# Block 0's second product: two of W_out's four slices as seven products of halves, and the first product in column halves

## The chip, the cores and the metric

The kernel runs on one core of a Trainium2 chip. The core has five engines that run side by side and wait for each other through semaphores: TensorE (PE in the profile; its weight loads are PEld), VectorE (DVE), ScalarE (ACT), GpSimd (POOL) and SyncE (SP), which here only issues DMAs. Each engine works through its own queue in order. The metric is the device time of one execution in microseconds.

## The reference

```python
# retention, for each of 4 batches x 8 heads, 768 tokens, head size 64
for t in range(S):
    state = gamma * state + outer(k[t], v[t])
    y[t] = scale * q[t] @ state
# then a feed-forward part over all 3072 tokens
x = y.transpose(0, 2, 1, 3).reshape(3072, 512)
h = x @ w_in                        # 512 -> 2048
g = h * tanh(softplus(h))           # the "mish" function
out = g @ w_out                     # 2048 -> 512, float32
```

Inputs and output are float32; the kernel computes its products on float16 copies.

## The kernel before

**Blocks.** The 3072 tokens are 24 chunks of 128. Block 0 has four chunks (512 tokens); every later block has two (256 tokens). For each block the kernel computes the retention part y, turns it into xt (the features on the partitions, the tokens in the columns), multiplies by W_in and applies mish (together `g1`), and multiplies by W_out. The retention part of the next block is computed by small products that are put between the large ones.

**Weights.** W_in and W_out arrive by DMA in four slices each, as float32, and are cast to float16 in SBUF. Slice s of W_out (`wout0` to `wout3`) holds the rows 512 s to 512 s + 511, as four row blocks of 128 (f = 0 to 3). The staging tiles are one ring of four buffers (tag "wt"): first the first q, then W_in's slices, then W_out's, and at last four tiles of sums, `tmat` (two) and `gsum` (two). Slices 0 to 2 of W_out are issued by `load_w`, one DMA of 1 MB each; slice 3 is issued in two halves by `load_last_wout`, out of `load_more`, after the loads of q, k and v for chunks 4 and 5. All of these stand in SP's queue in program order. `cast_wout` casts slices 0 to 2 on DVE (L220) and slice 3 on ACT in two halves (L218).

**Seven products.** From block 1 on, the second product is not computed plainly. Function `seven` splits the gate matrix g (256 tokens x 2048) and W_out (2048 x 512) into 2 x 2 parts each, a11 to a22 over halves of the tokens and of f, b11 to b22 over halves of f and of the columns. With s1 = a21 + a22, s2 = s1 - a11, s3 = a11 - a21, s4 = a12 - s2 and t1 = b12 - b11, t2 = b22 - t1, t3 = b22 - b12, t4 = b21 - t2, seven products (a11 b11, a12 b21, s1 t1, s2 t2, s3 t3, s4 b22, a22 t4) and some additions give the four parts of the result that eight products give otherwise. DVE makes the sums of g for each block (`gsum`, L699 to L708); the sums of the weights (`tmat`, `weight_sums`, L683 to L686) are made once, in two halves: half 0 from slices 0 and 2, half 1 from slices 1 and 3. In block 0 the kernel before makes them, but doesn't use them.

**Block 0.** Its order is written out by hand in the loop at L1076 and the dictionary `plan`: steps u = 0 to 15 are the first product, one row block of 128 of the 2048 features each. `open_in` does the first two; `g1` (L628) does the others with four products of 512 columns each (L635), and ACT applies mish on the finished bank (L643). Steps 16 to 31 are the second product: 64 products of 512 columns (`g2_mm`, L649), for each of 16 row blocks f one for each of the four token chunks t. Each of four PSUM banks (`o_ps`) gathers the sum of one token chunk over all of f. `g2_out` copies the banks out, bank 0 on ACT (L662), the others on DVE (L664), and the stores are issued in block 1.

Between them `plan` puts chunks 4 and 5 (called pair 2): `cast_qk` scales q and v on POOL (L297) and k on ACT (L293); `turn_two` turns q and k by 16 TensorE transposes (L247) into one PSUM tile, which DVE copies out in four pieces (L253); `pair_scores` does the scores of half the heads, twice, each with 16 small products (L327) and a mask on DVE (L332); `outer_two` does the outer products k v (L345) and the state (L358); `present_two` and `y_two` give y (L373, L383), whose two halves are copied to xt by DVE (L402) and ACT (L400). With that xt, block 1's first product starts. `turn_both` scales chunks 6 and 7 on POOL (L414, L417, L424), and SP turns them by DMA (L429) for block 1's small products.

PSUM has eight banks: four for the large products (one "px", three "mm") and two double ones ("at") for pair 2.

Of the kernel before, what the change touches and what calls it, by code (L numbers as in the profile page):

```python
# [9 lines left out]
FP16 = mybir.dt.float16  # L10
# [6 lines left out]
def kernel(  # L17
# [12 lines left out]
    P = 128  # L30
# [169 lines left out]
    def cast_win(s, by_tile=False):  # L200
        src = wtmps.pop(("in", s))
        wins[s] = []
        for j in range(2):
# [7 lines left out]
            wins[s].append(t)  # L211

    def cast_wout(s, on_act=False):
        src = wtmps.pop(("out", s))
        t = cpool.tile([P, FPS, d_model], FP16, name=f"wout{s}")
        if on_act:
            for f in range(0, FPS, 2):
                nc.scalar.copy(t[:, f:f + 2], src[:, f:f + 2])  # L218
        else:
            nc.vector.tensor_copy(t, src)  # L220
        wouts[s] = t

# [405 lines left out]
    def g1(blk, u):  # L628
# [3 lines left out]
        for j in range(per):  # L632
            s, f = divmod(u * per + j, FPS)
            for bp in range(NBP):
                nc.tensor.matmul(  # L635
                    h_ps[:, j], wins[s][f // 2][:, bp, f % 2 * P:(f % 2 + 1) * P], xts[blk][:, bp, :nt],
                    start=(bp == 0), stop=(bp == NBP - 1))
        room = NFB * TB // (2 * nt)
# [7 lines left out]

    def g2_mm(o_ps, blk, t, fb, cols=slice(None)):
        s, f = divmod(fb, FPS)
        nc.tensor.matmul(  # L649
            o_ps, gts[blk, fb][:, t * P:(t + 1) * P], wouts[s][:, f, cols],  # L650
            start=(fb == 0), stop=(fb == NFB - 1))

    def out_rows(blk, t):
# [4 lines left out]

    def g2_out(o_ps, t, due):
        osb = op.tile(list(o_ps.shape), FP32, name="osb", tag="osb")  # L660
        if t == 0:
            nc.scalar.copy(osb, o_ps)  # L662
        else:
            nc.vector.tensor_copy(osb, o_ps)  # L664
        stores.append((due, out_rows(0, t), osb))

    def weight_sums(half):
# [10 lines left out]
        t3, t4 = tmats[1][:, 0, f], tmats[1][:, 1, f]  # L678
        b11, b12 = wouts[half][:, :, :hf], wouts[half][:, :, hf:]
        b21, b22 = wouts[half + 2][:, :, :hf], wouts[half + 2][:, :, hf:]  # L680
        sub = ALU.subtract
# [28 lines left out]
    def in_sums(j):  # L710
        t = cpool.tile([P, 4, 2, TB // 2], FP16, name=f"wsum_{j}")
        wsums.append(t)
        (a11, a12), (a21, a22) = [(x[:, :2], x[:, 2:]) for x in (wins[0][j], wins[2][j])]
# [247 lines left out]
    def first_block():  # L961
# [82 lines left out]
        def turn_two():  # L1044
# [15 lines left out]

        plan = {
            9: [(cast_wout, 0)],
            12: [(cast_wout, 1)],
            16: [(cast_wout, 2), (load_more,), (cast_qk,)],
            17: [(sum_weights, 0, 3)],
            23: [(cast_wout, 3, True)],
            25: [(turn_two,)],
            26: [(pair_scores, 2, 0)],
            27: [(pair_scores, 2, 1)],
            28: [(sum_weights, 0, 1), (turn_both, CPB + 2)],  # L1070
            29: [(outer_two,)],
            30: [(present_two,), (sum_weights, 1, 1)],
            31: [(y_two,)],
        }
        o_tiles = [None] * CPB
        for u in range(2 * NFB):  # L1076
            if u < 2:
                if u == 0:
                    open_in(2)
            elif u < NFB:  # L1080
                g1(0, u)
            elif u < 2 * NFB - 2:
                w = u - NFB
                if w == 0:
                    for t in range(CPB):
                        pool, tag = (pxps, "px") if t == 0 else (mmps, "mm")
                        o_tiles[t] = pool.tile([P, d_model], FP32, name="o_ps", tag=tag)
                for t in range(CPB):
                    if t == CPB - 1 and w == 1:
                        g2_mm(o_tiles[t], 0, t, 0)  # L1090
                    if t < CPB - 1 or w > 0:
                        g2_mm(o_tiles[t], 0, t, w)
            else:
                for t in range(CPB // 2) if u % 2 == 0 else range(CPB // 2, CPB):
                    for w in range(NFB - 2, NFB):
                        g2_mm(o_tiles[t], 0, t, w)
                    g2_out(o_tiles[t], t, 0)
            for fn, *args in plan.get(u + 1, ()):
                fn(*args)

# [171 lines left out]
```

## Time and profile before

| | us |
|---|---|
| median of 3 runs | 196.34 (196.23 to 196.53) |
| the profiled execution | 196.27 |
| its span, first to last instruction | 194.5 |
| TensorE busy | 189.6 |
| granted TensorE clock, mean | 0.998 |
| block 0's first product in `g1`, 56 products | 19.34 to 31.42 |
| block 0's second product, pair 2 in it | 31.42 to 48.74 |

In the profile a row gives the start in us from the span's beginning, the time it took, the engine, the line in the kernel, the operation, the tiles it writes and reads, their shapes, how many instructions are merged in the row, and in square brackets the idle time before it with what ended it. TensorE pipelines its products: a row of 512 columns reads 380 ns, but the next starts 216 ns later, so costs are taken from start to start.

### The profile page before, as it was taken

How to read it: one execution, taken by the hardware profiler on the slowest of the kernel's cores; microseconds unless marked ns; L12 is line 12 of the kernel's file. 1: busy time of each engine (PE TensorE's matmuls, PEld its weight loads, DVE VectorE, ACT ScalarE, POOL GpSimd, SP SyncE). 2: the span in 40 equal slices, each digit the busy share in tenths (PEclk: the TensorE clock that was granted, in tenths of full speed). 3: DMA queues.
4: the chain of work that ended last, by engine and by line, in shares of the span. 5: the costliest groups of instructions: out<-in, count | busy, mean ns of one | idle time of the engine just before them, and what ended most of it. 6: DMA issues, size and time to landing. Idle time of an engine off the chain costs nothing.

```text
span 194.5 us, 6886 instructions
## 1 busy us (share of the span) xinstructions
PE 189.6 (97%) x2996; PEld 154.0 (79%) x2996; DVE 128.7 (66%) x248; ACT 99.5 (51%) x183; POOL 73.3 (38%) x96
## 2 busy tenths in 40 slices
PE   7998999999999999999999999999999999999994
PEld 7756444454888888888888888998998998988983
DVE  0796535889767378467884864965885885876462
ACT  3375764243553552554364364584574663763750
POOL 5262000549508746562826605525625700000000
PEclk9999999999999999999999999999999999999999
DMA  5999999999999999999999999889996250300202
GB/s 172 304 309 349 368 386 366 293 302 202 202 260 248 157 233 225 214 175 216 261 207 227 278 192 287 103 225 245 77 223 123 50 150 5 111 0 20 95 27 81
DMA packets 84285, 38.75 MB, mean 199 GB/s; under 512 B 57760, under 2 KB 78880, under 8 KB 84256
## 3 DMA queue, kind: packets, MB, share of 16 engines
q1 hardware_dynamic: 84112, 38.28, 84.7%
q8 instruction: 23, 0.38, 0.9%
q10 hardware_dynamic: 144, 0.05, 0.1%
q14 instruction: 6, 0.05, 0.1%
HBM read 27.31 MB, written 6.29 MB: 173 GB/s over the span
## 4 chain that ended last, share of the span: by engine, by line
PE 93%; DMA 3%; ACT 1%; DVE 1%; issue 1%; SPq 0%
PE o_ps L838 32%; PE h_ps L635 24%; PE h_ps L765 9%; PE h_ps L745 8%; PE o_ps L649 7%; PE y_ps L551 3%; DMA qfirst<-in_q_dram 3%; PE u_ps L479 1%; PE at L472 1%; PE t_ps L247 1%; PE y_ps L373 1%; PE h_ps L620 1%; PE at L443 1%; PE at L327 1%; DVE qk L259 1%
## 5 line engine op out<-in xcount | busy, mean ns | idle before, releaser
L635 PE MATMUL h_ps<-xt,win 128*128 128x256 f16 (+1 forms) x376 | 48.5, 289 | 0.0
L635 PEld LDWEIGHTS <-win 128*128 128x128 f16 x376 | 36.5, 98 | 10.4 <-issue 0.2
L643 ACT ACTIVATE g<-h_ps 128x512 f16<-128x512 f32 x54 | 32.2, 597 | 23.7 <-PE h_ps L635 23.7
L838 PEld LDWEIGHTS <-gsum 128*128 128x128 f16 x320 | 30.3, 98 | 3.8
L838 PE MATMUL o_ps<-tmat,gsum 128*128 128x256 f16 x240 | 29.8, 273 | 0.0
L838 PEld LDWEIGHTS <-g 128*128 128x128 f16 x248 | 23.4, 98 | 2.7
L853 DVE TENSOR_TENSOR osb<-o_ps,snap 128x256 f32<-128x256 f32 (+1 forms) x33 | 13.8, 418 | 14.0 <-PE o_ps L838 8.9
L844 ACT COPY snap<-o_ps 128x256 f32<-128x256 f32 (+1 forms) x33 | 12.2, 370 | 20.7 <-PE o_ps L838 20.7
L414 POOL TENSOR_TENSOR qk<-qf,qvs 128x512 f16<-128x512 f32 x18 | 19.2, 1065 | 4.8 <-DMA qf<-in_q_dram 4.7
L765 PE MATMUL h_ps<-xt,win 128*128 128x256 f16 x160 | 20.7, 273 | 0.0
L424 POOL TENSOR_TENSOR v<-vf,qvs 128x512 f16<-128x512 f32 x18 | 19.7, 1101 | 1.2 <-DMA vf<-in_v_dram 1.0
L417 POOL TENSOR_TENSOR qk<-kf,qvs 128x512 f16<-128x512 f32 x18 | 19.1, 1060 | 2.7 <-DMA kf<-in_k_dram 2.6
L838 PE MATMUL o_ps<-wout,g 128*128 128x256 f16 x160 | 19.1, 273 | 0.0
L1179 POOL COPY summed<-gsum 128x1 f16<-128x1 f16 x7 | 3.0, 432 | 37.2 <-DVE gsum L704 29.8
L765 PEld LDWEIGHTS <-win 128*128 128x128 f16 x160 | 14.8, 98 | 1.4
L756 ACT ACTIVATE g<-h_ps 128x512 f16<-128x512 f32 x25 | 14.2, 588 | 2.4 <-PE h_ps L765 2.4
L600 ACT CAST xt<-y_ps 128x512 f16<-128x512 f32 x15 | 10.2, 734 | 10.2 <-PE y_ps L551 10.2
L649 PE MATMUL o_ps<-wout,g 128*128 128x512 f16 x64 | 15.0, 380 | 0.0
L780 DVE TENSOR_TENSOR hsum<-h_ps,hsum 128x512 f32<-128x512 f32 x15 | 10.4, 692 | 6.1 <-PE h_ps L745 4.4
L775 ACT COPY hsum<-h_ps 128x512 f32<-128x512 f32 x15 | 8.8, 585 | 10.5 <-PE h_ps L745 10.5
L699 DVE TENSOR_TENSOR gsum<-g 128x512 f16<-128x512 f16 x20 | 9.2, 459 | 5.2 <-ACT g L643 3.1
L507 DVE TENSOR_TENSOR mid<-u_ps,sth 128x256 f16<-128x256 f32 x15 | 6.3, 422 | 8.5 <-PE u_ps L479 8.2
(99 smaller groups left out, 277.7 us busy)
## 6 DMA issues: line engine op xcount, KB each, us to landing
kf<-in_k_dram SPq DMA_DIRECT2D x24, 256.0 KB, 5.3
vf<-in_v_dram SPq DMA_DIRECT2D x24, 256.0 KB, 5.5
out_dram<-osb SPq DMA_DIRECT2D x22, 256.0 KB, 3.5
qf<-in_q_dram SPq DMA_DIRECT2D x20, 256.0 KB, 4.3
wi<-in_moe_w_in_dram SPq DMA_DIRECT2D x6, 512.0 KB, 8.7
wt<-in_moe_w_out_dram SPq DMA_DIRECT2D x3, 1024.0 KB, 10.3
qfirst<-in_q_dram SPq DMA_DIRECT2D x2, 512.0 KB, 4.6
wi<-in_moe_w_in_dram SPq DMA_DIRECT2D x1, 1024.0 KB, 10.0
```

The costliest lines, as they stand in the source:

```text
L414: nc.gpsimd.tensor_tensor(in_place(q16.rearrange("p (w x) d -> p w x d", x=2)), by_head(qf), scale_by_head(qs_two[:, heads]), op=ALU.mult)
L417: nc.gpsimd.tensor_tensor(k16.rearrange("p (y w) d -> p w y d", y=2), kf.rearrange("p (w y) d -> p w y d", y=2), boosts.rearrange("p (w y) ...
L424: nc.gpsimd.tensor_tensor(cast[g][2], loaded.pop(g)[2], vs[g % 2].unsqueeze(2).broadcast_to((P, H, D)), op=ALU.mult)
L635: nc.tensor.matmul(h_ps[:, j], wins[s][f // 2][:, bp, f % 2 * P:(f % 2 + 1) * P], xts[blk][:, bp, :nt], start=(bp == 0), stop=(bp == NBP - 1))
L643: nc.scalar.activation(gt, h_ps, AF.Mish, scale=inv_boost3)
L649: nc.tensor.matmul(o_ps, gts[blk, fb][:, t * P:(t + 1) * P], wouts[s][:, f, cols], start=(fb == 0), stop=(fb == NFB - 1))
L745: nc.tensor.matmul(o_ps[:, f], w(f // 2, k)[:, f % 2 * P:(f % 2 + 1) * P], x[:, k], start=begin and f == 0 and k == 0, stop=k == 1, skip_g ...
L756: nc.scalar.activation(to, src, AF.Mish, scale=inv_boost3)
L765: nc.tensor.matmul(h_ps[:, f], wins[w][h // 2][:, k, h % 2 * P:(h % 2 + 1) * P], xts[blk][:, k, :2 * C], start=k == 0, stop=k == NBP - 1)
L838: nc.tensor.matmul(o_ps[:, cols], x(f), w(f)[:, cols], start=first and z == 0, stop=z == n - 1, skip_group_check=True)
L844: nc.scalar.copy(x, o_ps[:, cols])
L853: nc.vector.tensor_tensor(dst, o_ps[:, cols], plus, op=ALU.add)
```

## The change

Block 0's second product takes another form, with what serves it:

- `g1` issues its products in pieces of 256 columns. For later blocks, whose tiles are 256 wide, that is what it was; in block 0 each product becomes two, each with its own weight load.
- Slices 0 and 2 of W_out (f blocks 0 to 3 and 8 to 11) are multiplied by seven products, over halves of f (slice 0, slice 2), halves of the tokens (two chunks each) and halves of the columns. Slices 1 and 3 are multiplied plainly, in pieces of the same size. Every product or piece is 8 instructions of 256 columns (4 row blocks x 2 chunks).
- A PSUM bank now holds two chunks x 256 columns. Parts that are used twice are copied or added out of PSUM on the way (`kept_sum`: m1 and m5 on ACT, u2 and u3 on DVE), and u3 + m5 is formed on POOL (u35). The results are written out in halves by `done`.
- DVE makes the four sums of the gates (`first_sums`), two of them before W_out's first cast. The weight sums of half 0 are spread over the second product; those of half 1 stay at its end.
- Slice 2 of W_out is loaded by two DMAs and cast in two halves.
- `turn_two` copies its four pieces out on ACT, not on DVE.
- The steps of pair 2 stand in another order among the large products, written out in `first_out`; the two score steps follow each other.

```diff
@@ load_w
-            if s < NSL - 1:
+            if s == NSL - 2:
+                for f in range(0, FPS, FPS // 2):
+                    at = s * FPS + f
+                    nc.sync.dma_start(t[:, f:f + FPS // 2], wout_ap[:, at:at + FPS // 2])
+            elif s < NSL - 2:
                 nc.sync.dma_start(t, wout_ap[:, s * FPS:(s + 1) * FPS])
@@ cast_wout
-        if on_act:
+        if s >= NSL - 2:
             for f in range(0, FPS, 2):
-                nc.scalar.copy(t[:, f:f + 2], src[:, f:f + 2])
+                (nc.scalar.copy if on_act else nc.vector.tensor_copy)(t[:, f:f + 2], src[:, f:f + 2])
@@ g1
-                nc.tensor.matmul(
-                    h_ps[:, j], wins[s][f // 2][:, bp, f % 2 * P:(f % 2 + 1) * P], xts[blk][:, bp, :nt],
-                    start=(bp == 0), stop=(bp == NBP - 1))
+                for at in range(0, nt, 2 * C):
+                    cols = slice(at, at + 2 * C)
+                    nc.tensor.matmul(
+                        h_ps[:, j, cols], wins[s][f // 2][:, bp, f % 2 * P:(f % 2 + 1) * P],
+                        xts[blk][:, bp, cols], start=(bp == 0 and at == 0), stop=(bp == NBP - 1),
+                        skip_group_check=blk == 0)
@@ new
+    def first_sums():
...
+        lo, hi = gtiles[0, 0][:, :FPS], gtiles[0, 1][:, :FPS]
+        n = TB // 2
...
+            lambda: nc.vector.tensor_tensor(s3, lo[:, :, :n], lo[:, :, n:], op=sub),
+            lambda: nc.vector.tensor_tensor(s1, lo[:, :, n:], hi[:, :, n:], op=add),
+            lambda: nc.vector.tensor_tensor(s2, s1, lo[:, :, :n], op=sub),
+            lambda: nc.vector.tensor_tensor(s4, hi[:, :, :n], s2, op=sub),
...
+    def kept_sum(src, plus=None):
+        m = op.tile([P, *src.shape[1:]], FP32, name="hsum", tag="hsum", bufs=6)
+        if plus is None:
+            nc.scalar.copy(m, src)
+        else:
+            nc.vector.tensor_tensor(m, src, plus, op=ALU.add)
+        return m
...
+        def mm(ij, x, w, fs=range(FPS)):
+            for f in fs:
+                for t in range(2):
+                    nc.tensor.matmul(
+                        banks[ij][:, t], x(f)[:, t * P:(t + 1) * P], w(f), start=ij in open_banks,
+                        stop=f == fs[-1], skip_group_check=True)
...
+        mm((0, 0), a(0, 0), b(0, 0))
+        m1 = kept_sum(banks[0, 0])
+        mm((0, 1), s(1), t(1))
+        m5 = kept_sum(banks[0, 1])
+        load_more()
+        cast_qk()
+        plain(1, 1, 1)
+        plain(0, 0, 1)
+        weight(0, 1)
+        mm((0, 0), a(0, 1), b(1, 0))
+        mm((0, 1), s(4), b(1, 1))
+        mm((1, 0), s(2), t(2))
+        u2 = kept_sum(banks[1, 0], m1)
+        weight(0, 2)
+        plain(0, 1, 1)
+        turn_two()
+        cast_wout(3, True)
+        mm((1, 0), s(3), t(3))
+        u3 = kept_sum(banks[1, 0], m1)
+        u35 = op.tile([P, 2, hf], FP32, name="hsum", tag="hsum", bufs=6)
+        nc.gpsimd.tensor_tensor(u35, u3, m5, op=ALU.add)
+        pair_scores(2, 0)
+        pair_scores(2, 1)
+        turn_both(CPB + 2)
+        mm((1, 0), a(1, 1), t(4))
+        plain(1, 0, 1)
+        for j in (1, 0):
+            plain(0, j, 3, range(2))
+        outer_two()
+        plain(0, 1, 3, range(2, FPS))
+        done(0, 1, u2)
+        plain(0, 0, 3, range(2, FPS))
+        done(0, 0)
+        present_two()
+        weight(1, 1)
+        plain(1, 0, 3)
+        y_two()
+        done(1, 0, m1)
+        plain(1, 1, 3)
+        done(1, 1, u35)
...
@@ turn_two
-                    taken(pairs[2, nm + "t"][:, i], t_ps[:, j, i], False)
+                    taken(pairs[2, nm + "t"][:, i], t_ps[:, j, i], True)
@@ first_block, in place of plan and the loop over 2 * NFB
+        for u in range(NFB):
+            if u == 0:
+                open_in(2)
+            elif u > 1:
+                g1(0, u)
+            if u == 2 * FPS + FPS - 1:
+                sums, make = first_sums()
+                make[0]()
+                make[1]()
+                cast_wout(0)
+                sum_weights(0, 1)
+                make[2]()
+                cast_wout(1)
+                make[3]()
+                cast_wout(2)
+        first_out(load_more, cast_qk, turn_two, sums, sum_weights)
```

In `first_out`, `plain(i, j, n)` adds slice n's share to the part with token half i and column half j, `a`, `b`, `s` and `t` pick the operands of the seven products, and `weight(half, n)` is `sum_weights`, which makes the next n of the four weight sums.

More of the change, by code (lines that the diff above doesn't have):

```diff
@@ new lines, in win_sum_tile, with first_out, a, b @@
+    def win_sum_tile(j):
+        while len(wsums) <= j:
+            wsums.append(cpool.tile([P, 4, 2, TB // 2], FP16, name=f"wsum_{len(wsums)}"))
+        return wsums[j]
+    def kept_sum(src, plus=None):
+        m = op.tile([P, *src.shape[1:]], FP32, name="hsum", tag="hsum", bufs=6)
+        if plus is None:
+            nc.scalar.copy(m, src)
+        else:
+            nc.vector.tensor_tensor(m, src, plus, op=ALU.add)
+        return m
+    def first_out(load_more, cast_qk, turn_two, sums, weight):
+        hf = d_model // 2
+        banks = {(0, 0): pxps.tile([P, 2, hf], FP32, name="o_ps", tag="px")}
+        for ij in ((0, 1), (1, 0), (1, 1)):
+            banks[ij] = mmps.tile([P, 2, hf], FP32, name="o_ps", tag="mm")
+        open_banks = set(banks)
+        osb = [op.tile([P, d_model], FP32, name="osb", tag="osb") for _ in range(CPB)]
+        def mm(ij, x, w, fs=range(FPS)):
[4 more added lines that the diff above has]
+                        stop=f == fs[-1], skip_group_check=True)
+                    open_banks.discard(ij)
+        def a(i, j):
+            return lambda f: gts[0, 2 * j * FPS + f][:, i * 2 * P:(i + 1) * 2 * P]
+        def b(i, j):
+            return lambda f: wouts[2 * i][:, f, j * hf:(j + 1) * hf]
+        def s(i):
+            return lambda f: sums[i - 1][:, f]
+        def t(i):
+            return lambda f: tmats[(i - 1) // 2][:, (i - 1) % 2, f]
+        def plain(i, j, n, fs=range(FPS)):
+            mm((i, j), lambda f: gts[0, n * FPS + f][:, i * 2 * P:(i + 1) * 2 * P],
+               lambda f: wouts[n][:, f, j * hf:(j + 1) * hf], fs)
+        def done(i, j, plus=None):
+            for n in range(2):
+                dst, src = osb[2 * i + n][:, j * hf:(j + 1) * hf], banks[i, j][:, n]
+                if plus is None:
+                    nc.scalar.copy(dst, src)
+                else:
+                    nc.vector.tensor_tensor(dst, src, plus[:, n], op=ALU.add)
+        mm((0, 0), a(0, 0), b(0, 0))
[38 more added lines that the diff above has]
+        done(1, 1, u35)
+        for n in range(CPB):
+            stores.append((0, out_rows(0, n), osb[n]))
@@ L678, in weight_sums @@
         t3, t4 = tmats[1][:, 0, f], tmats[1][:, 1, f]
[L679 to L680 removed]
+        (b11, b12), (b21, b22) = [
+            (w[:, :, :hf], w[:, :, hf:]) for w in (wout_tile(half), wout_tile(half + 2))]
         sub = ALU.subtract
```

64 lines of the change are left out of this document (11 added, 53 removed).

## The prediction

> **What bounds the kernel now.** I read the page first, then the chain of waits for block 0 in order of time, then the timeline of the same stretch, engine by engine.
>
> ```profile
> PE 189.6 (97%) x2996; PEld 154.0 (79%) x2996; DVE 128.7 (66%) x248; ACT 99.5 (51%) x183; POOL 73.3 (38%) x96
> PE 93%; DMA 3%; ACT 1%; DVE 1%; issue 1%; SPq 0%
> ```
>
> The chain that ended last lies on TensorE for 93%. What block 0 gains or loses on TensorE is passed on to the end.
>
> ```profile
> 31.59 7.77 PE o_ps L649 x36
> 39.36 0.89 PE t_ps L247 x16
> 40.25 0.86 PE o_ps L649 x4
> 41.11 0.40 PE at L327 x16
> 41.52 0.97 PE o_ps L649 x4
> 42.49 0.35 PE at L327 x16
> 42.84 1.83 PE o_ps L649 x8
> ```
>
> Columns: start, length, piece. The second product (L649) runs without a hole; the small attention products (L247 transposes, L327 scores) lie between pieces of it. Nothing here is a long wait.
>
> ```profile
> 12.02 0.63 ACT L293 ACTIVATE v<-vf 128x512 f16<-128x512 f32 x1
> 12.55 0.58 ACT L251 COPY qkt<-t_ps 128x512 f16<-128x512 f16 x1
> ...
> 32.09 1.23 DVE L220 CAST wout<-wt 128x2048 f16<-128x2048 f32 x1 [1.49 <-DMA wt<-in_moe_w_out_dram]
> 34.86 1.23 DVE L220 CAST wout<-wt 128x2048 f16<-128x2048 f32 x1 [1.55 <-DMA wt<-in_moe_w_out_dram]
> 35.88 2.56 POOL L297 TENSOR_TENSOR qk<-qf,qvs 128x512 f16<-128x512 f32 x2 [18.05 <-DMA qf<-in_q_dram]
> 36.01 1.53 DVE L683 TENSOR_TENSOR tmat<-wout 128x1024 f16<-128x1024 f16 x1
> 37.57 1.42 DVE L684 TENSOR_TENSOR tmat<-wout,tmat 128x1024 f16<-128x1024 f16 x1
> 39.28 2.21 POOL L297 TENSOR_TENSOR v<-vf,qvs 128x512 f16<-128x512 f32 x2 [0.84 <-DMA vf<-in_v_dram]
> 40.09 1.03 PE L649 MATMUL o_ps<-wout,g 128*128 128x512 f16 x4
> 40.29 1.42 DVE L253 COPY qkt<-t_ps 128x512 f16<-128x512 f16 x4 [0.70 <-PE t_ps L247]
> 42.77 1.90 PE L649 MATMUL o_ps<-wout,g 128*128 128x512 f16 x8
> 48.74 5.40 PE L635 MATMUL h_ps<-xt,win 128*128 128x256 f16 x48
> 56.50 1.91 PE L838 MATMUL o_ps<-wout,g 128*128 128x256 f16 x16
> 58.25 1.91 PE L838 MATMUL o_ps<-tmat,gsum 128*128 128x256 f16 x16
> 59.99 1.04 PE L838 MATMUL o_ps<-wout,gsum 128*128 128x256 f16 x8
> ```
>
> What to see: the slices of W_out arrive just ahead of their use and are cast on arrival (32.09, 34.86). DVE's subtractions (L683, L684) last 1.5 us beside POOL's scalings, against 0.68 us for L685 alone. DVE empties the transposes in four copies at 0.33 us pitch; one such copy takes ACT 0.58 us. Block 1 begins at 48.74.
>
> **Products.** From starts, 56 of L635's 512-column products take 31.42 - 19.34 = 12.08, 0.2158 us each; the 256-column ones 3.49 / 32 = 0.1091 (56.50 to 59.99), with a weight load each.
> - First product in halves: 56 x (2 x 0.1091 - 0.2158) = +0.13.
> - Second product: 64 x 0.2158 = 13.81 becomes seven products of 8 and eight plain pieces of 8, 120 x 0.1091 = 13.09: -0.72.
>
> **Waits before the scores.** TensorE would start the second product at 31.42 + 0.13 = 31.55. I walk DVE's new queue: s3 (0.69, row L704) after W_in's last cast ends at 28.0; s1 when the twelfth gate tile is out of ACT (28.77 + 0.1); cast 0 29.5 to 30.74; t1 to 31.46; s2 to 32.1; cast 1, arrival-bound as before, 32.09 to 33.32; s4 to 33.9. TensorE is through products 1 and 5 at 31.55 + 16 x 0.1091 = 33.30 and waits for cast 1 (33.32 + 0.05) 0.07 us. Slice 2 is now cast in halves (0.69 each, row L210): the second, on arrival, 34.86 to 35.55; TensorE wants it after 20 more products, at 35.55: 0.05. Together +0.12. t2 follows from 35.59 to 36.27, wanted at about 36.9; t3 after u2, to 39.3, wanted at 39.55. Product 1's copies (m1, m5) lie on an idle ACT. So the transposes end at 35.60 + 28 x 0.1091 + 0.89 = 39.55 (40.09 before).
>
> **The scores.** Here two covers go. Before, between transposes and first scores lay four wide products (0.86), between the two scores four more; now eight narrow ones (0.87) and none. And the four copies move from DVE to ACT, because DVE has t4 and u3 there. They start 0.20 after the transposes (40.09 to 40.29); on ACT each takes 0.585 and the next starts 0.48 later, as the L293 row overlaps its successor by 0.10. Scores 0 need two copies: 0.20 + 0.48 + 0.585 + 0.05 to TensorE = 1.32 after the transposes. Scores 1 need four: 2.28; with 0.35 of their own they end at 2.63. Before: 42.77 - 40.09 = 2.68, of it eight products at 0.2158 = 1.73, so 0.95 of other time; now 2.63 - 0.87 = 1.76. That is +0.81, with one change between big and small tiles already saved in it (about 0.1 us on each side: 0.97 against 0.86 for four products). What is late next: scores end at 39.55 + 2.63 = 42.18. u3, which must empty the bank that product a22 t4 writes, waits for t4: POOL's first v scaling holds it to 40.33, it ends 0.55 later (below), u3 by 41.6. It is covered.
>
> **The rest.** Remaining: 48 x 0.1091 = 5.24, and the other time of that stretch, 48.74 - 42.77 - 20 x 0.2158 = 1.66, as before: block 1 starts at 49.08, +0.34. Costed at nothing:
> - The added DMA issue (slice 2 in two, L192, 0.37 us each): SP's next issues take up to 2.5 us each on a full queue, which swallows it. If not, q, k, v and slice 3 come 0.4 late; slice 3's second cast (43.83) is wanted at 45.3.
> - ACT: slice 3's casts stand behind the four copies, which end near 41.8, against an arrival at 41.37; wanted at 43.9.
> - POOL's new u35 (about 1.04, row L414): between the last v scaling (41.9) and block 1's q scaling, which waits for its DMA until 43.83; behind it stand those casts, SP's transposes and block 1's small products at 54.07.
> - DVE's late emptying: block 1's second tile needs u=(1,0) out of its bank at about 49.7; TensorE asks at 49.95. Without that margin, 0.1 to 0.3.
>
> Sum: +0.13 - 0.72 + 0.12 + 0.81 = **+0.34 us**. The profiled execution took 196.27 (span 194.5 and 1.8 around it), so 196.61; on the median 196.34, 196.68. I say **196.65**. Unseen before is the ACT copy chain at this place: its bounds are DVE's pitch of 0.33 (copies done 1.0 us sooner) and 0.585 without overlap (0.3 later). I take the overlapped ACT row, of the same form and engine.
>
> **Rival 1, the lock, slower.** L683 ended at 37.54, 0.55 after POOL's first scaling (36.99); L684 at 38.99, 0.55 after the second (38.44). A subtraction begun during a POOL scaling thus seems to do nothing until that ends. t2 starts at 35.59, POOL at 35.88: 0.3 us decide. If t2 comes second it ends at 37.54, and product s2 t2 waits 0.7; u2 ends at 39.35, t3 then falls behind the v scaling and ends at 40.87, which delays s3 t3 by another 0.7 at most; t4 ends near 42.45, u3 at 43.15, so a22 t4 starts at 43.2 instead of 42.2. +1.0 more: **197.6**. For it: the margin is one DMA's jitter. Against it: both starts hang on neighbouring transfers of one queue.
> [...]
>
> **Rival 2, the scores don't wait.** If q's copies start after q's own eight transposes, or ACT is quicker, the 0.81 shrinks. For: q and k lie in different banks. Against: at 40.29 DVE, free since 39.6, started its q copy only after the last k transpose. Without the wait, u3 sets the next start, 41.6 against 42.18: +0.34 - 0.56, **196.1**. If t4 also gets ahead of the v scaling (both come up at 39.3), u3 ends at 41.3: **195.8**.
>
> **Rival 3, it doesn't save.** 232 narrow products each carry a weight load of 98 ns on 109. Were the pitch 0.115 here, +1.4: **198**. All 256-column rows, with DVE and ACT busy beside them, speak against it.
>
> **How the numbers follow.** Forecast 0.58, own range 196.35 to 197.0; rival 1 0.16; rival 2 0.22, half at each price; rival 3 0.04. A measurement of this kernel tells about 0.2% (0.39 us) from no change, so the forecast itself straddles 196.73: some 0.25 of its 0.58 lies above, and with rivals 1 and 3 slower gets 0.45. Faster is the lower half of rival 2 and a little more, 0.13. The rest, 0.42, is no change. Range 196.0 to 197.4: it leaves out 195.8 and the dear end of rival 1.
>
> **What would show it.** Right: block 1's first product at about 49.1; TensorE idle some 0.3 and 0.7 us ahead of the two scores, released by ACT; narrow products at 0.109; t2 at 0.68. Rival 1: t2 over 1.2 us and holes ahead of s2 t2 and s3 t3. Rival 2: scores back to back after s3 t3. Wrong altogether if a hole opens elsewhere, ahead of slice 1 or 3, or if block 1 does not carry the shift to the end.

## The result, and the profile after

The changed kernel takes **197.71 us** (median of 6 runs, 197.39 to 198.49); the kernel before, run beside it, 196.30 (196.23 to 196.53). The ratio is 1.0078, 95% interval [1.0057, 1.0098]: slower by 1.1 to 1.9 us. Here and below, medians, ranges and ratios leave out executions more than 1.5% above the fastest of the same kernel (three of six of `e3_fewer_instr`, two of six of `e4_more_instr`, one of twelve of `e10_two_banks`). The prediction was 196.65 with a range up to 197.4; the time lies above the range.

The profiled execution took 197.66 us with a span of 195.54; before, 196.27 and 194.49. The chain of waits of block 0, in order of time (start, length, piece), of the changed kernel:

```profile
19.48 2.07 PE h_ps L645 x19
21.55 0.59 issue
22.14 10.31 PE h_ps L645 x93
32.46 6.99 PE o_ps L702 x64
39.44 0.91 PE t_ps L255 x16
40.35 0.02 issue
40.37 2.06 ACT qkt L259 x4
42.44 0.04 issue
42.48 0.42 PE at L335 x16
42.90 2.74 PE o_ps L702 x24
```

Three things are to be seen. The first product (L645) is now in two parts, and between them lie 0.59 us of "issue", time in which the engine waited for nothing that the profile shows. The second product's 64 narrow products ahead of the transposes take 6.99 us without a gap. And ScalarE's four copies (L259) stand on the path between the transposes and the second scores, as forecast.

The timeline around the first of these, of the changed kernel (start, length, engine, line, operation, in brackets the idle time before it and what ended that):

```profile
19.31 2.24 PE L645 MATMUL h_ps<-xt,win 128*128 128x256 f16 x19
...
22.14 2.13 PE L645 MATMUL h_ps<-xt,win 128*128 128x256 f16 x18 [0.59 <-issue]
22.14 1.95 PEld L645 LDWEIGHTS <-win 128*128 128x128 f16 x18 [0.77 <-issue]
```

and of the kernel before, at the same place:

```profile
19.34 4.91 PE L635 MATMUL h_ps<-xt,win 128*128 128x512 f16 x22
```

Products and weight loads stop together, in the middle of a gate tile, after 19 products, and no semaphore lets them go on. By starts the gap is 21.28 to 22.14, so 0.75 us more than a pitch of 0.109.

The scores' stretch, of the changed kernel:

```profile
39.16 2.49 POOL L305 TENSOR_TENSOR v<-vf,qvs 128x512 f16<-128x512 f32 x2 [0.80 <-DMA vf<-in_v_dram]
39.29 1.47 DVE L792 TENSOR_TENSOR tmat<-wout,wout 128x1024 f16<-128x1024 f16 x1
40.37 2.05 ACT L259 COPY qkt<-t_ps 128x512 f16<-128x512 f16 x4 [1.47 <-PE t_ps L255]
40.80 1.03 PE L702 MATMUL o_ps<-tmat,wsum 128*128 128x256 f16 x8 [0.47 <-DVE tmat L792]
42.48 0.26 PEld L335 LDWEIGHTS <-qkt 64*64 64x64 f16 x16 [0.46 <-ACT qkt L259]
```

t3 (L792) did fall behind GpSimd's first v scaling, which ended at 40.21: t3 ended 0.55 later, and its product waited 0.47. But that wait is under the four copies, which hold the second scores until 42.48 in any case.

Term by term, in us (execution against execution):

| term | forecast | measured |
|---|---|---|
| first product, by pitch | +0.13 | +0.14 |
| hole in the first product | 0 | +0.75 |
| second product, by pitch | -0.72 | -0.71 |
| waits for W_out | +0.12 | 0 |
| scores and copies | +0.81 | +0.85 |
| other time up to block 1 | 0 | -0.06 |
| block 1's start (48.743 to 49.712) | +0.34 | +0.97 |
| from there to the end of the span (145.75 to 145.83) | 0 | +0.08 |
| time less span (1.78 to 2.12) | 0 | +0.34 |
| sum | +0.34 | +1.39 |

Two terms that the prediction didn't have make the miss: the hole, and 0.34 us outside the span, which all six runs of the changed kernel show (2.08 to 2.16).

### The profile page after: what moved, and what is told of

Read it like the earlier page. It is cut to its first block, busy times and chain, and to the rows that moved or that the text cites. A ratio compares the mean times of both kernels' runs of the same rounds, so it can differ in the third digit from the quotient of the medians.

```text
span 195.5 us, 7129 instructions
## 1 busy us (share of the span) xinstructions
PE 188.3 (96%) x3108; PEld 164.1 (84%) x3108; DVE 128.6 (66%) x254; ACT 102.5 (52%) x190; POOL 73.7 (38%) x97
## 4 chain that ended last, share of the span: by engine, by line
PE 92%; DMA 3%; ACT 2%; issue 1%; DVE 1%; SPq 0%
PE o_ps L944 32%; PE h_ps L645 24%; PE h_ps L871 9%; PE h_ps L851 8%; PE o_ps L702 6%; PE y_ps L559 3%; DMA qfirst<-in_q_dram 3%; PE u_ps L487 1%; PE at L480 1%; ACT qkt L259 1%; PE t_ps L255 1%; PE y_ps L381 1%; PE h_ps L628 1%; PE at L451 1%; PE at L335 1%
## 5 line engine op out<-in xcount | busy, mean ns | idle before, releaser
L645 PE MATMUL h_ps<-xt,win 128*128 128x256 f16 x432 | 48.8, 273 | 0.6 <-issue 0.6
L645 PEld LDWEIGHTS <-win 128*128 128x128 f16 x432 | 42.0, 98 | 5.7 <-issue 0.8
L871 PE MATMUL h_ps<-xt,win 128*128 128x256 f16 x160 | 20.7, 273 | 0.0
L871 PEld LDWEIGHTS <-win 128*128 128x128 f16 x160 | 14.8, 98 | 1.4
L851 PE MATMUL h_ps<-xt,wsum 128*128 128x128 f16 x160 | 11.4, 219 | 0.0
```

The lines of the kernel that those rows point to most:

```text
L645: nc.tensor.matmul(h_ps[:, j, cols], wins[s][f // 2][:, bp, f % 2 * P:(f % 2 + 1) * P], xts[blk][:, bp, cols], start=(bp == 0 and at == 0) ...
L851: nc.tensor.matmul(o_ps[:, f], w(f // 2, k)[:, f % 2 * P:(f % 2 + 1) * P], x[:, k], start=begin and f == 0 and k == 0, stop=k == 1, skip_g ...
L871: nc.tensor.matmul(h_ps[:, f], wins[w][h // 2][:, k, h % 2 * P:(h % 2 + 1) * P], xts[blk][:, k, :2 * C], start=k == 0, stop=k == NBP - 1)
```

## The experiments

**The theories.** Theory S: TensorE ran out of instructions. The page's table of DMA queues has a queue of kind "instruction" (packets, MB, share). Before:

```profile
q8 instruction: 23, 0.38, 0.9%
```

After:

```profile
q8 instruction: 24, 0.39, 0.9%
```

The trace gives each of these packets as 16384 bytes (16 KiB). TensorE's trace counts 5998 instructions before and 6222 after, products and weight loads together; divided by 256 that is 23.4 and 24.3. So each packet should be a block of 256 of TensorE's instructions (64 bytes each): an estimate from these counts. By S such blocks end behind TensorE's instructions 449, 705 and so on, 256 apart, where the gaps stand. Of these places the kernel before has 22 and the changed kernel 23; TensorE passes them within 0.21 us, from start to start, but for one in the kernel before (a gap of 0.61 us at 15.4) and two in the changed one (0.53 there, and the 0.86 here). In both kernels one such packet starts at 19.6 us; in the changed kernel TensorE stops when it has begun 705 instructions (the expectations below say the 704th), at 21.28, and the kernel before begins its 705th at 23.22. Halves use up two instructions per 0.109 us in place of 0.216, and so, by S, reach the end of the block before the next one is there.

The gap that the kernel before has already stands 256 instructions earlier, behind 449, in its timeline:

```profile
15.42 0.25 PE L373 MATMUL y_ps<-am,v 64*64 64x128 f16 x3 [0.40 <-issue]
```

With that the step can be reckoned. In the changed kernel TensorE goes through instructions 449 to 705 from 15.39 to 21.28, in 5.89 us. The packet at 19.57 starts 4.18 after the first of these, takes 1.15, and TensorE goes on 1.42 later: 6.75 us, and the difference is the gap of 0.86. In the kernel before the same instructions last from 15.42 to 23.22, 7.80 us, and there is no gap.

Rival A: narrow products, or their accumulation flags, have a cost of their own. Rival B: the new order or the loads of the second product stall the first. (The first expectations below call any late data, such as a cast or a bank, theory D.)

### Each half of the change alone

The first kernel undoes the first product's division and keeps the rest; the second is the kernel before with that division alone (the same edit the other way round).

```diff
--- changed kernel, g1 (e1_wide_first: undone)
-                for at in range(0, nt, 2 * C):
-                    cols = slice(at, at + 2 * C)
-                    nc.tensor.matmul(
-                        h_ps[:, j, cols], wins[s][f // 2][:, bp, f % 2 * P:(f % 2 + 1) * P],
-                        xts[blk][:, bp, cols], start=(bp == 0 and at == 0), stop=(bp == NBP - 1),
-                        skip_group_check=blk == 0)
+                nc.tensor.matmul(
+                    h_ps[:, j], wins[s][f // 2][:, bp, f % 2 * P:(f % 2 + 1) * P], xts[blk][:, bp, :nt],
+                    start=(bp == 0), stop=(bp == NBP - 1))
```

> The changed kernel with block 0's first product in 512 columns again; all else as changed. Its trace has a hole of 0.76 us on TensorE at 21.3 us, inside the first product, that no semaphore explains. Theory S (supply): TensorE had run out of fetched instructions, as narrow products use up two instructions in 0.109 us where wide ones take 0.216; so the hole goes, the first product takes 12.08 us instead of 12.98, the two waits for W_out that I had counted (0.12) come back, block 1 starts 0.2 us later than before (49.0), and the time is 196.5 to 196.9. Theory D (data): the hole is a late cast or bank of W_in's slices; then some hole of 0.5 us or more stays between 19.3 and 31.4, and the time is 197.3 or more.

> The kernel before with only the column halves of block 0's first product. S and D alike: the hole comes, 0.5 to 1.0 us near 21.3, the first product takes about 13.0 us, and nearly all of the loss is here: 197.1 to 197.5. If instead the new order of the second product makes the loss (my forecast's score term alone), this kernel takes 196.3 + 0.13 = 196.4 to 196.5.

Measured: 201.03 us for the wide first product (200.62 to 202.10, 6 runs; ratio 1.0238 [1.0211, 1.0265]) and 201.29 for the narrow one alone (199.54 to 202.41, 6 runs; 1.0241 [1.0201, 1.0280]). At the disputed place both came out as S has it: undivided, the first product runs 12.09 us without a hole; divided alone, it has a gap of 0.65 behind instruction 705 (gaps here from start to start, so with a pitch in them). That leaves rival B out. But both times missed by about 4 us. In both traces gaps without a semaphore stand at new places far behind block 0, behind instruction 4289 (1.06 in both) and 4801 (0.96 and 1.00). 705, 4289 and 4801 lie whole multiples of 256 apart (4289 - 705 = 14 x 256, 4801 - 705 = 16 x 256). A third new gap, behind 3179 (0.88 and 0.75), is of another kind: there TensorE waits for one of the DMAs that turn q and k (`qkt`). Each half alone shifts all later instructions by 112; both together by 224, which is 32 short of 256. So S grew a second half: what counts for the rest of the program is **which instructions the block boundaries fall on**.

### Shifting the boundaries only

Two kernels that change nothing but the number of warm-up products at the start, whose results nobody reads: the changed kernel with 34 fewer of them, each wider (68 instructions fewer), and the kernel before with 46 more, each half as wide (92 more).

```diff
--- changed kernel, first_block (e3_fewer_instr)
-        spin(46, 1)
+        spin(46)
--- kernel before, spin (e4_more_instr)
+        if n == 46:
+            for i in range(2 * n):
+                nc.tensor.matmul(
+                    to[:, 0, 0, :C // 2], ident, ident[:, :C // 2], start=True, stop=True)
+            return
```

> The changed kernel, narrow first product kept; only the 46 warm-up products of 128 columns ahead of the first transposes become 12 of up to 512 columns: the same columns, 68 TensorE instructions fewer before 6 us. S: TensorE reaches the end of what is fetched 68 instructions (3.7 us of narrow products) later, after the fetch has landed, so the hole at 21.3 goes or shrinks below 0.2 us; 196.8 to 197.1. D, or any cause that lies in the narrow products themselves: hole and time as changed, 197.5 to 198.

> The kernel before, wide first product; only the 46 warm-up products become 92 of 64 columns: the same columns, 92 TensorE instructions more before 6 us. S: a hole without a semaphore appears between 18 and 22 us, where the kernel before has none, of 0.3 to 3 us, and the time grows by as much. D: no hole, 196.3 within 0.3.

Measured: 202.23 (200.47 to 203.30, 3 runs; ratio 1.0278 [1.0228, 1.0327]) and 207.51 (205.99 to 208.73, 4 runs; 1.0554 [1.0502, 1.0606]). Fewer instructions did take the hole at 21.3 away, but put a worse one elsewhere, which the expectation missed. More instructions brought the hole about where it was expected, but cost 11 us and not the 0.3 to 3 of the hole alone. The chain of waits of the kernel with fewer:

```profile
15.48 0.19 PE u_ps L353 x21
15.67 2.87 issue
18.54 0.26 PE u_ps L353 x9
```

and of the kernel with more:

```profile
17.86 0.11 PE y_ps L383 x5
17.97 1.90 issue
19.87 0.53 PE y_ps L383 x9
```

The gaps stand in the midst of attention's small products, behind instruction 449 (705 - 256) and 705. The instruction packets from the trace, beside the gaps:

```
                       packet          TensorE stops  goes on   on after the packet's end
kernel before          12.91 - 14.10       14.81       15.42        1.32
changed kernel         19.57 - 20.72       21.28       22.14        1.42
e3_fewer_instr         15.97 - 17.05       15.47       18.54        1.49
e4_more_instr          17.20 - 18.32       17.75       19.87        1.55
```

Four times TensorE resumes 1.3 to 1.6 us after the end of such a packet. That ties the gap to the packet, not to any data. It holds far beyond these four. Pair the packets of a trace, in order, with the places behind TensorE's instructions 449, 705, 961 and so on. Over the traces of all 18 kernels of this case that gives 410 pairs. In none does TensorE pass the place sooner than 1.29 us after the end of its packet. Of 27 gaps of 0.3 us or more at these places, 26 have no semaphore, and all 26 end 1.29 to 1.60 us after their packet; the other one waits for VectorE. What sets the start of a packet stays open: here it is 4.18 us after TensorE has passed the place before, in the median of a trace about 1 us.

### Two tests of S against its rivals

The first keeps the arithmetic of the change and its narrow products, but puts them late in the first product, where by S the next block of instructions has come (its packet ended at 20.72 in the changed kernel); the second adds 256 instructions, a whole block, to the kernel before, by division alone.

```diff
--- changed kernel, g1 (e5_late_narrow)
+                wide = 2 * C if blk else 4 * C if u < 9 else 2 * C if u < 12 else C
-                for at in range(0, nt, 2 * C):
-                    cols = slice(at, at + 2 * C)
+                for at in range(0, nt, wide):
+                    cols = slice(at, at + wide)
--- kernel before, g1 and g2_mm (e6_whole_page)
+                wide = 2 * C if blk else 4 * C if u < 10 else 2 * C if u < 11 else C
...
+        for at in (0, hf):
             nc.tensor.matmul(
-                o_ps, gts[blk, fb][:, t * P:(t + 1) * P], wouts[s][:, f, cols],
+                o_ps[:, at:at + hf], gts[blk, fb][:, t * P:(t + 1) * P], wouts[s][:, f, at:at + hf],
```

> Edit: the first product's tiles 2 to 8 keep 512-wide products, tiles 9 to 11 have halves, tiles 12 to 15 quarters: 60 products more than the undivided form where the change has 56, so that the later instructions lie nearly as they do in the changed kernel (8 further on), but the 704th instruction of TensorE is reached at about 23.4 us instead of 21.3. Theory S (TensorE runs out of instructions at 704 since halves use them up too fast, and everything else in the program depends on where the boundaries every 256 instructions fall): no hole of over 0.3 us between 20 and 24 us, first product about 12.3 us long, block 1 starts at 48.9 to 49.3, time 196.7 to 197.2. Rival A (narrow products have a cost of their own beside their pitch): first product 12.9 or longer, time 197.6 or more. Rival B (any change of the number of instructions costs several us, wherever the boundaries lie): 200 or more.

> Edit, on the kernel before: 128 further products, that is 256 further instructions of TensorE, by division alone: the first product's tile 10 in halves, tiles 11 to 15 in quarters, and all 64 products of the second product in halves. No arithmetic, load or copy is changed. Theory S: the boundaries after block 0 fall on the same instructions as before, the 704th is reached in time, so no new hole; only the pitch of the narrow products is paid (about 0.3 to 0.4 us) and perhaps one further fetch: 196.5 to 197.2. Rival B (the number of instructions itself costs, as it did for the kernels with 92 to 156 more): 200 or more, with holes at later boundaries.

Measured: late narrow products 197.20 (197.01 to 198.22, 6 runs; ratio 1.0054 [1.0034, 1.0075]); a whole block more 196.57 (196.26 to 196.60, 12 runs; 1.0009 [1.0000, 1.0017]). The chain with late narrow products:

```profile
19.48 12.24 PE h_ps L646 x116
31.71 6.99 PE o_ps L703 x64
```

and with a whole block more on the kernel before:

```profile
19.50 12.25 PE h_ps L638 x120
31.75 7.86 PE o_ps L655 x72
```

116 and 120 products in one piece each, at their pitch; no hole. 256 further instructions cost 0.30 us up to block 1's start, the narrow products' pitch, and 0.01 behind it, where 92 to 156 further ones had cost 1.6 to 8.3 us behind it. Most of the 8.3 is six gaps at such places in `e4_more_instr`, 7.1 us together (its granted clock was 0.992 against 0.998 before, by estimate some 1 us more). The 1.6 is no such gap: in `e3_fewer_instr` TensorE waits 1.5 us at 123.3 for a DMA that turns q and k, as it does for a shorter time behind 3179 in the two kernels above. Why that DMA is late in these three isn't shown.

| kernel | instructions more than before | to the nearest multiple of 256 | block 1 starts | from there to the span's end |
|---|---|---|---|---|
| before | 0 | 0 | 48.74 | 145.75 |
| e6_whole_page | 256 | 0 | 49.04 | 145.76 |
| changed | 224 | -32 | 49.71 | 145.83 |
| e5_late_narrow | 232 | -24 | 48.96 | 145.94 |
| e1_wide_first | 112 | 112 | 49.51 | 149.33 |
| e2_narrow_only | 112 | 112 | 49.59 | 149.33 |
| e3_fewer_instr | 156 | -100 | 52.71 | 147.31 |
| e4_more_instr | 92 | 92 | 52.86 | 154.04 |

Rival A (first product 12.9 or longer) and the count of instructions as a cost of its own both fall.

### The 0.34 us outside the span

One load of slice 2 in place of two; eight more small copies on ScalarE in the kernel before (248 instructions in its record for 239; the changed kernel has 247); one more small memset on GpSimd in the changed kernel; two more on VectorE in the changed kernel; six and nine more on VectorE in the kernel before.

```diff
--- kernel before (f4_dve_nine_more; the others likewise)
-    nc.vector.memset(warm, 0.0)
+    for _ in range(10):
+        nc.vector.memset(warm, 0.0)
```

> Edit: the changed kernel with W_out's slice 2 loaded by one DMA again instead of two. The time less the span of TensorE and the others is 1.77 us before and 2.1 to 2.2 us after the change. If the further DMA makes that, it falls back to 1.75 to 1.9 us and the time to about 197.3; if the other engines' longer programs make it, or their work at the end, it stays at 2.05 to 2.25. The hole at the 704th instruction stays in either case (0.5 to 1 us).

> Edit, on the kernel before: eight copies of one element on ScalarE at its very start, where it has 5 us of nothing to do, and nothing else. ScalarE's record then counts 247 instructions as in the changed kernel (before 239). What is open: the time less the span is 1.77 us before and 2.1 to 2.2 with the change; it went back to 1.8 in the kernel with t3 early, where ScalarE counts 245. If ScalarE's length makes it: time less span 2.05 to 2.25, span as before, time 196.5 to 196.9. If not: 1.70 to 1.85 and 196.2 to 196.5.

> Edit: the changed kernel with two further one-element memsets on VectorE at the start, nothing else. The time less the span is 2.08 to 2.16 in all runs of the changed kernel, where VectorE's record counts 311 instructions, and 1.73 to 1.85 in the kernels with 302 (before) and 313 (t3 early, two banks). If VectorE's length makes it: 1.7 to 1.9 here (313). If not: 2.05 to 2.2.

> Edit: the kernel before with six further one-element memsets on VectorE at the start, nothing else; its program then has as many instructions as the changed kernel's. If VectorE's length makes the 0.35 us outside the span: time less span 2.05 to 2.2 here. If not: 1.7 to 1.9.

> Edit: the changed kernel with one further one-element memset on GpSimd at the start, nothing else (the kernel with t3 early had one more there too). If GpSimd's length makes it: time less span 1.7 to 1.9. If not: 2.05 to 2.2.

> Edit: the kernel before with nine further one-element memsets on VectorE at the start, so that VectorE's record counts 311 instructions as in the changed kernel (308 in the run with six more, 302 before). If just that length of VectorE's stream makes the 0.35 us outside the span: time less span 2.05 to 2.2. If it takes something else of the change besides: 1.7 to 1.85.

The record counts an engine's semaphore and drain instructions too, which the page leaves out (VectorE before: 248 on the page, 51 and 3 more in the record).

| kernel | VectorE's instructions in its record | time less span, us (runs) | median time |
|---|---|---|---|
| before | 302 | 1.73 to 1.85 (27) | 196.51 |
| changed | 311 | 2.08 to 2.16 (6) | 197.71 |
| e8_one_load | 311 | 2.08 to 2.17 (6) | 197.74 |
| f3_pool_one_more | 311 | 2.08 and 2.15 (2) | 198.02 |
| f1_dve_two_more | 313 | 1.75 to 1.79 (5) | 197.56 |
| e9_act_longer | 302 | 1.73 to 1.81 (12) | 196.52 |
| f2_dve_six_more | 308 | 1.74 to 1.81 (8) | 196.77 |
| f4_dve_nine_more | 311 | 2.06 to 2.18 (8) | 196.82 |

Neither the further load nor ScalarE's or GpSimd's length makes it: f1 has both at the changed kernel's 247 and 155, and the short time. The medians of f2 and f4 are too close to tell this (before, beside them, 196.43 and 196.48; ratios 1.0014 [0.9990, 1.0039] and 1.0015 [0.9999, 1.0032]), as the spans move by more from run to run; the time less span does. The hole was in e8's, f1's and f3's traces as in the changed kernel's (0.75). Nine one-element memsets on VectorE, which only set one element again to the value that it has, bring it into the kernel before in every one of 8 runs, and two further ones take it out of the changed kernel. All kernels of this case keep to it: in the eight with 311 the time less span is 2.06 to 2.24 in every run, in the ten with 302, 308 or 313 it is 1.73 to 1.91. Other lengths weren't run. Why a stream of 311 costs 0.34 us and one of 308 or 313 doesn't is open: what happens there lies outside what the profiler recorded.

### The scores' wait, and a version without the two costs

The next kernel takes late narrow products and attacks the copies: t3 directly behind t2, t4 ahead of the copies, k's copies on VectorE, GpSimd's v scalings behind t4.

```diff
--- with late narrow products, first_out and turn_two (e7_t3_early)
-        weight(0, 1)
+        weight(0, 2)
         mm((0, 0), a(0, 1), b(1, 0))
...
-        weight(0, 2)
+        weight(0, 1)
+        nc.gpsimd.tensor_copy(summed, t(4)(FPS - 1)[:, hf - 1:])
+        cast_v()
...
-                    taken(pairs[2, nm + "t"][:, i], t_ps[:, j, i], True)
+                    taken(pairs[2, nm + "t"][:, i], t_ps[:, j, i], nm == "q")
```

> Edit: as the kernel with late narrow products, and the scores' wait is attacked: the sum t3 directly behind t2, t4 ahead of the copies, the two k copies on VectorE beside ScalarE's two q copies, GpSimd's two v scalings held back until t4 is done. Theory (the scores' wait is ScalarE's row of four copies): the wait of 0.45 us ahead of the second scores and most of the 0.6 us ahead of them go, block 1 starts 0.4 to 0.8 us earlier than in the kernel with late narrow products, time 196.0 to 196.8, at or a little below the kernel before. Rival (VectorE becomes the bound there: t4, two copies, u3 in one row): the wait moves to the products behind the scores and the time stays within 0.2 us of the kernel with late narrow products.

Measured: 197.05 (196.90 to 198.81, 11 runs; ratio 1.0044 [1.0021, 1.0066]), 0.15 below late narrow products though the time less span alone came down by 0.3 (to 1.8; VectorE counts 313 here). Within the span nothing was gained: the rival's time, and in its last step the rival's cause. The chain:

```profile
38.75 0.91 PE t_ps L255 x16
39.66 0.02 issue
39.68 0.59 ACT qkt L259
40.27 0.02 issue
40.30 0.43 DVE qkt L261
40.73 0.02 issue
40.75 0.59 ACT qkt L259
41.35 0.02 issue
41.37 0.04 DVE qkt L261
41.41 0.30 issue
41.71 0.69 DVE hsum L688
```

The copies on the two engines follow one another, each released by the other's: all read one PSUM tile. So VectorE's second copy ends only at 41.80, u3 (L688) stands behind it on VectorE, and the product behind the scores waits 0.25 for u3. TensorE gets there 2.97 us after the transposes (2.66 with ScalarE alone); without u3 it would be about 2.7, no better than ScalarE alone. So the next kernel gives q and k a PSUM tile each, and has 72 products more than the undivided first product, so that all later instructions lie exactly 256 further on; beside it, the kernel with late narrow products aligned in the same way.

```diff
--- turn_two (e10_two_banks, with the edit above)
-            t_ps = atps.tile([P, 2, HP, 2, C], FP16, name="t_ps", tag="at")
+            t_ps = [atps.tile([P, HP, 2, C], FP16, name="t_ps", tag="at") for _ in "qk"]
--- g1 (e10_two_banks and e11_aligned)
-                wide = 2 * C if blk else 4 * C if u < 9 else 2 * C if u < 12 else C
+                wide = 2 * C if blk else 4 * C if u < 8 else 2 * C if u < 11 else C
```

> Edit: as the kernel with t3 early, but the transposes of q and of k go to two tiles of PSUM instead of one, so that ScalarE's and VectorE's copies needn't follow one another; and the first product is divided into 72 products more than the undivided form (tiles 8 to 10 halves, 11 to 15 quarters), so that with the second product's 56 the later instructions lie 256 further on, exactly as before. Theory: the copies end about 1.1 us after the transposes instead of 2.2, the second scores end 1.8 to 2.3 us after the transposes' end (2.63 forecast, 2.68 measured in the changed kernel, 2.97 in the kernel with t3 early), block 1 starts at 48.3 to 48.7, time less span 1.75 to 1.85, time 196.0 to 196.5. Rival (t4, u3 and the sums behind the scores are late instead): block 1 at 48.9 or later, 196.7 or more.

> Edit: as the kernel with late narrow products, but with 72 products more than the undivided form instead of 60 (tiles 8 to 10 halves, 11 to 15 quarters), so that the later instructions lie exactly 256 further on than before, instead of 232. Theory S: block 1 starts within 0.1 us of the kernel with late narrow products (48.96), what comes behind it takes as long as before (145.75 us; 145.94 there), span 194.7 to 194.9, time 196.8 to 197.0 with 2.1 outside the span. Rival (what lies behind block 1's start is longer for another reason, such as the later loads): 145.9 or more again, 197.1 to 197.3.

Measured: two banks 196.25 (195.79 to 198.30, 11 runs; ratio 0.9987 [0.9960, 1.0013]); aligned 197.55 (197.04 to 198.54, 10 runs; 1.0060 [1.0036, 1.0083]). The timeline with two banks:

```profile
39.53 1.07 ACT L259 COPY qkt<-t_ps 128x512 f16<-128x512 f16 x2
39.98 0.76 DVE L261 COPY qkt<-t_ps 128x512 f16<-128x512 f16 x2 [0.41 <-PE t_ps L255]
40.75 0.64 PE L335 MATMUL at<-qkt 64*64 64x128 f16 x32
41.60 1.03 PE L703 MATMUL o_ps<-tmat,g 128*128 128x256 f16 x8 [0.21 <-DVE hsum L688]
```

The copies overlap and both scores run back to back; TensorE is past them 1.82 us after the transposes (39.78) in place of 2.68, and what it waits for then, 0.21, is u3 on VectorE. Block 1 starts at 48.46, 0.3 ahead of the kernel before. In the time that is not told apart from the kernel before; the changed kernel (ratio 1.0078 [1.0057, 1.0098]) it beats.

The aligned kernel missed its expectation: block 1 started at 49.44, not 48.96. Its first product began 0.23 late (19.57), and a wait of 0.17 for the cast of W_out's slice 1 stood ahead of that slice. Behind block 1's start it took 145.86, so the residue of 0.1 to 0.2 in the table isn't the alignment alone.

The last kernel is the change with its arithmetic, loads and order, without the two costs: late narrow products, and two more memsets on VectorE.

> Edit: the kernel with late narrow products (no hole at the 704th instruction) and two further one-element memsets on VectorE at the start (no 0.35 us outside the span): the change with its arithmetic, loads and order as they are, without the two costs that the prediction didn't have. If these two are what it missed: block 1 starts at 48.9 to 49.3, time less span 1.7 to 1.85, time 196.6 to 197.1 (the prediction was 196.65). If there is a third cost: 197.2 or more.

Measured: 197.23 (197.00 to 197.50, 10 runs; ratio 1.0034 [1.0022, 1.0045]), time less span 1.75 to 1.82, block 1 at 49.34: just above what was expected for two costs, and in the range given for a third. Its chain:

```profile
21.67 10.68 DMA wt<-in_moe_w_out_dram
32.35 0.02 issue
32.37 1.24 DVE wout L230
33.61 0.05 issue
33.65 5.43 PE o_ps L704 x48
```

Here TensorE is on time again and waits 0.38 for cast 1, which waits for its load. That is a third term, and the hole had covered it: in the changed kernel TensorE came to that slice at 34.04, 0.12 after cast 1 ended (33.92). Without the hole the wait was 0 (late narrow products), 0.17 (aligned), 0.38 here and 0.70 (wide first product), by when the load lands.

## Why the prediction was wrong

- **The step that failed is "Products"**, "First product in halves: 56 x (2 x 0.1091 - 0.2158) = +0.13". The pitch was right (0.1092 in 112 products); what was left out is that 56 more products are 112 more instructions, used up at twice the rate (two in 0.109 us in place of 0.216). The step had no term for their supply. Undoing the division alone takes the hole away, dividing alone brings it, and dividing later avoids it (12.24 us, as the pitch has it): shown. That the hole is the wait for a block of instructions is inferred from the packets (size, spacing by 256, and 26 gaps in 18 traces that all end 1.29 to 1.60 us after their packet); no row of a trace names it.
- "(span 194.5 and 1.8 around it)" was held constant. It was 2.12. That VectorE's length of 311 instructions makes this is shown; why, is not.
- "Waits before the scores", +0.12, came to 0, because the hole had made TensorE late. Without the hole it is 0 to 0.70. The forecast lay inside this, but as one number for a load whose landing moves by half a microsecond it was too sure.
- The second product, -0.72, is right (-0.71).
- The scores, +0.81, are right in mechanism and size (+0.85). The forecast put a wait of about 0.3 ahead of the first scores; that didn't come, because s3 t3 waited 0.47 in its place.
- Rival 1 (t2 comes second): t2 got ahead of GpSimd by 0.03 us (35.77 against 35.80) and took 0.69; t3 did fall behind. It (L792) took 1.47 in place of t2's 0.69 and ended 0.55 after the scaling, as L683 and L684 did in the kernel before; the prediction calls this the lock. What makes it isn't shown. It cost nothing, being under the copies. Rival 1's price of 197.6 is near the result by luck; the reason is another.
- Rival 2 (scores don't wait) is refuted here, and its price is about what two PSUM tiles reach. Rival 3 (pitch 0.115) is refuted.
- What the prediction named as the sign of being wrong altogether, "a hole opens elsewhere", is what happened, if at another place than it named.

Without the two costs the change still costs 0.75 us of medians (f5: 197.23 against 196.48). In its trace block 1 starts 0.60 late: +0.15 pitch, -0.71 second product, +0.84 scores, +0.38 wait, -0.06 other; behind that it loses 0.09. So the sign of the forecast's +0.34 and four of its five terms stand; the wait for W_out was 0.26 too small for that execution.

## What to carry to other kernels

Count an engine's instructions as a resource like bytes: here a division that doubled them over the same work put a gap of 0.86 us behind TensorE's instruction 705, and the places where such gaps stood were fixed by the count from the program's start (449 and whole multiples of 256 further on). When a change adds or removes instructions on TensorE, compare with a version whose count differs from the old one by a multiple of 256, or its time may tell of the shift and not of the change (here up to 11 us). And a wait of 0 behind a new hole isn't a wait that was free: without the hole it was back here, at 0.17 to 0.70 us in three of the four kernels named above.

## What was not expected of the hardware

- Gaps of 0.3 to 3.1 us on TensorE without a semaphore, at instruction counts 256 apart, each ending 1.3 to 1.6 us after a packet of the instruction queue; the kernel before has one of 0.6 too. Shifts of 92 to 156 instructions left this kernel 4.5 to 11 us slower than before, a shift of 256 0.2.
- A VectorE stream of 311 instructions made the execution some 0.34 us longer outside the span than one of 302, 308 or 313 (2.06 to 2.24 us against 1.73 to 1.91).
- Copies on ScalarE and VectorE out of one PSUM tile ran one after the other, 0.56 us from start to start (39.68 to 41.37 in three steps); out of two tiles, one for each engine, they overlapped (39.53 to 40.60 and 39.98 to 40.74).
